# FFN-down of a gated spectral mixer: which chunks of the FFN rows lie in the large tile, and at which byte the tiles begin

## The chip, the cores and the metric

The kernel runs on one core of one Trainium2 chip. The metric is device time in microseconds (us), the median over several executions. The numbers below come from those executions and from one execution that the hardware profiler took.

## The reference

A spectral mixer `a` and a gated FFN `b` work on the same input `x` (2 batches, 4096 tokens, 640 features, float32), and a sigmoid gate per token mixes them.

```python
g = sigmoid((x * gate_w).sum(-1, keepdims=True))
a = irfft2(mlp(rfft2(x)))                               # 4 blocks of 160 features, soft threshold
b = (gelu(x @ w_gate) * (x @ w_up)) @ w_down            # 640 -> 1728 -> 640
return g * a + (1 - g) * b
```

The change lies in the last product of `b`, the FFN-down: for 8192 tokens, 1728 FFN rows are contracted to 640 features.

## The kernel before, in words

All products run on TensorE in a split form: a float32 operand is written as a high part (a copy by ScalarE, `high`, L285) and a rest (a subtraction on VectorE, `low`, L288), and a product is three matmuls: high x high, rest x high, high x rest. `split` does one of each. A matmul has a stationary operand, which is loaded into the array ahead of it, and a moving operand, which streams through. Matmuls that add into one PSUM bank follow one another; `run` (L473) issues those of the FFN and `mms`/`mm3` (L304) most others.

The program has four stretches: (1) FFN-up with gate (`quad`, 256 columns a matmul; between quads stand the steps of the first transform, `a_step`, L624); (2) the spectral MLP; (3) the inverse transforms; (4) the FFN-down with the second inverse transform (`inv2`) and the mixing. The order of the instructions is written out by hand: lists of hooks say between which matmul groups a load, a split or a sum is issued, and each engine works through its own in that order.

*FFN rows.* The 1728 rows are 14 chunks of 128, the last half filled (its other half is zero). `h_store` writes each chunk of the hidden values to a DRAM tensor `hD` with 14 columns of 128 for each token group, `h_load` reads them back in the FFN-down.

*The FFN-down* (`down`) uses a Strassen-like form with seven block products: chunk `j` is paired with `j + 6` for j below 6, and chunk 12 with 13. A unit `i` (32 of them) is two groups of 128 tokens. Each of its blocks, in the order a11, s2, s3, s1, a12, a22, s4, contracts seven chunks, j = 0 to 6, against weights of the forms b11, t2, t3, t1, b21, t4, b22. A chunk takes three matmuls of 320 columns (two for the half-filled j = 6 in a12, a22, s4, called `HALF`), so that a unit has 144.

The stationary operands are the tiles `ho`, which `h_op` makes two blocks ahead: five chunks in one `big` tile, two chunks in two `still` tiles. The five are chunks 0 to 4 (6 to 10), the two are 5 and 12 (11 and 13); the blocks take them in this order. The moving operands are the weights `wx`; `wd_load` brings them in pieces of four, three or two parts into `big`, `mid` and `small` tiles, where they stay.

*Pools.* For each partition, `small` has 17 tiles of up to 640 floats, `big` 17 of 1344, `still` 12 of 256, `mid` 13 of 1024, `tiny` 10. A `big` tile of `ho` uses 1280 of its 1344 floats and a `mid` tile of `wx` 960 of 1024, so that these may begin at an offset; `off` counts floats of 4 bytes. `small` and `still` are used in full by `wx` and `ho`. `off` is 15 for `wx` in `big`, 31 for `wx` and for the operands of `inv2` in `mid`, and 0 for `ho`. The seven weight sets take 14 of the 17 `big` tiles.

*First transform.* `f1_load` brings its tables into `big` tiles at offset 0. In `a_step` they are the stationary operand and `xs`, in a `small` tile, the moving one, 320 columns.

Of the kernel before, what the change touches and what calls it, by code (L numbers as in the profile page):

```python
# [11 lines left out]
F32R = mybir.dt.float32r  # L12
# [3 lines left out]
P = 128  # L16
# [198 lines left out]
def spectral_mix_kernel(ctx: ExitStack, tc: tile.TileContext, a):  # L215
# [3 lines left out]
    def dr(t, off, ap):  # L219
        return bass.AP(tensor=t.tensor, offset=t.offset + off, ap=ap)  # L220
# [11 lines left out]
    def small(shape, dt=F32, name="small"):  # L232
        return pool[0].tile(shape, dt, name=name, tag="small", bufs=17)

    def view(t, shape, off):

        n = math.prod(shape[1:])
        t = t[:, off:off + n]
        if len(shape) == 3:
            return t.rearrange("p (a b) -> p a b", a=shape[1])  # L240
        if len(shape) == 4:
            return t.rearrange("p (a b c) -> p a b c", a=shape[1], b=shape[2])
        return t

    def big(shape, dt=F32, name="big", off=0):
        return view(pool[1].tile([P, 1344], dt, name=name, tag="big", bufs=17), shape, off)

    def still(shape, dt=F32, name="still"):
        return pool[2].tile(shape, dt, name=name, tag="still", bufs=12)
# [4 lines left out]
    def tiny(shape, dt=F32, name="tiny"):  # L254
        return pool[5].tile(shape, dt, name=name, tag="tiny", bufs=10)

    ld = nc.sync.dma_start
    late = []

    def st(dst, src):  # L260
        late.append((dst, src))
# [11 lines left out]
    hD = dram.tile([64, P, 14 * P], F32, name="hD")  # L273
# [10 lines left out]
    def high(dst, src, scale=1.0):  # L284
        nc.scalar.activation(dst, src, AF.Copy, scale=scale)  # L285

    def low(dst, src, hi, eng=nc.vector):
        eng.tensor_sub(dst, src, hi.bitcast(F32))  # L288

    def split(dst_h, dst_l, src, eng=nc.vector):  # L290

        high(dst_h, src)
        low(dst_l, src, dst_h, eng)
# [177 lines left out]
    def run(dst, ops, first=True):  # L471
        for i, (l, r) in enumerate(ops):
            nc.tensor.matmul(dst, l, r, start=first and i == 0, stop=i == len(ops) - 1, skip_group_check=True)  # L473

    def h_store(tp, t, h):
        st(dr(hD, 4 * tp * P * 14 * P + t * P, [[14 * P, P], [P * 14 * P, 4], [1, P]]),
           h.rearrange("p (t n) -> p t n", t=4))

    def x_of(o, *names):
# [11 lines left out]
    def quad(key, t, hook, fresh):  # L491
# [50 lines left out]
        def half4():  # L542
            run(C, prod(w["u2"], x_of(o, "t4")), first=False)
            nc.vector.tensor_add(u2, C, u2)  # L544
            h = v["h"]
            nc.vector.tensor_mul(h[:, 256:], h[:, 256:], v["u4"])
            nc.vector.tensor_mul(h[:, :256], u2, p1)
            h_store(key[1], t, h)
# [34 lines left out]
    F1, XR, XS, GW = {}, {}, {}, []  # L583

    def f1_load(q):
        m = min(5, 17 - 5 * q)
        F1[q] = big([P, 5, 2, P], F32R, name="f1")
        for x in (slice(0, 1), slice(1, m)):
            nc.gpsimd.dma_start(F1[q][:, x], a["f1"][:, 5 * q + x.start:5 * q + x.stop])

# [426 lines left out]
    V, WM, S2, HR, HO = {}, {}, {}, {}, {}  # L1017
    HALF = ("a12", "a22", "s4", "b21", "t4", "b22")
# [67 lines left out]
    def wd_load(j, part):  # L1086
        d = WM.setdefault(j, {})
        kinds = {(5, 2): ((big, 4), (small, 2)), (6, 1): ((small, 2),) * 2, (6, 2): ((small, 2),) * 3}.get(
            (j, part), (((big, 4),) if part < 2 else ((mid, 3),) * 2))
        at_, parts = 4 * part, []  # L1090

        def go(t, k, n):
            ld(t.rearrange("p h d -> p (h d)").bitcast(F32), dr(wdf[j], 320 * k, [[14 * 320, P], [1, 320 * n]]))
        for i, (kind, n) in enumerate(kinds):
            off = {} if kind is small else {"off": 31} if kind is mid else {"off": 15}
            t = kind([P, n, 320], F32R, name="wx", **off)
            if part < 2 or i == 0:
                go(t, at_, n)
            else:
                later.append(lambda t=t, k=at_, n=n: go(t, k, n))  # L1100
            parts += [t[:, k] for k in range(n)]
            at_ += n
        for k in range(len(parts) // 2):
            d[FORMS[2 * part + k]] = parts[2 * k], parts[2 * k + 1]
# [17 lines left out]
    def h_load(i, part):  # L1122

        b, na = c_seq[i]
        d = HR.setdefault(i, {})
        for r, k in (((0, 0), (1, 0)), ((1, 1), (0, 1)))[part]:
            blk = (32 * b + toks(na)[r]) * P * 14 * P
            t, u = small([P, 5, P], name="hraw"), tiny([P, 2, P], name="hraw")
            d[f"a{r + 1}{k + 1}"] = t, u
            ld(t, dr(hD, blk + 6 * k * P, [[14 * P, P], [1, 5 * P]]))  # L1130
            ld(u, dr(hD, blk + (6 * k + 5) * P, [[14 * P, P], [(7 - 5 * k) * P, 2], [1, P]]))

    def h_s3(i, eng=nc.vector):
        d = HR[i]
# [20 lines left out]
        d["s4"] = d.pop("s2")  # L1155

    def h_op(i, name, eng=nc.vector):
        t = big([P, 5, 2, P], F32R, name="ho")
        uh, ul = (still([P, 2, P], F32R, name="ho") for k in range(2))
        src, six = HR[i].pop(name) if name in ("s1", "s3", "s4", "a22") else HR[i][name]  # L1160
        split(t[:, :, 0], t[:, :, 1], src, eng)
        if name == "a22":
            high(uh[:, 0], six[:, 0])
            high(ul[:64, 1], six[:64, 1])
            high(uh[64:, 1], six[:64, 1])
            low(ul[:, 0], six[:, 0], uh[:, 0], eng)
            low(uh[:64, 1], six[:64, 1], ul[:64, 1], eng)
        elif name in HALF:
            high(uh, six)
            low(ul[:, 0], six[:, 0], uh[:, 0], eng)  # L1170
            low(uh[64:, 1], six[:64, 1], uh[:64, 1], eng)
        else:
            high(uh, six)
            low(ul, six, uh, eng)
        HO[i, name] = [(t[:, j, 0], t[:, j, 1]) for j in range(5)] + [(uh[:, j], ul[:, j]) for j in range(2)]

    def inv2(i):

# [156 lines left out]
    for k, (b, n2) in enumerate(a_seq):  # L1335
        i, j = steps_a[k]
        sp = A_POINTS[keys[i][0]][j]
        if k == 0:
            back(i, sp[0] - 12, lambda: f1_load(0))
        back(i, sp[0] - 9, lambda b=b, n2=n2: a_load(b, n2))  # L1340
        for s, f in zip(sp, (lambda b=b, n2=n2: a_split(b, n2, 0), lambda b=b, n2=n2: a_split(b, n2, 1),
                             lambda b=b, n2=n2: a_gate(b, n2), lambda b=b, n2=n2: a_step(b, n2, 0),
                             lambda b=b, n2=n2: a_step(b, n2, 1))):
            back(i, s, f)
        if k in (17, 37, 57):
            back(i, sp[4], lambda q=(k + 3) // 20: f1_load(q))
# [24 lines left out]
    for i, key in enumerate(keys):  # L1371
        gr, tp = key
# [3 lines left out]
        if nxt:  # L1376
# [3 lines left out]
            for k, s in enumerate((5, 8, 11, 14, 16, 18, z + 1, z + 4, z + 6) if gr < 2 else  # L1380
                                  (6, 9, 13, 17, 21, z + 1, z + 2, z + 3, z + 3, z + 5)):
                if k < 9 or nxt[0] == 2:
                    f0, f1, f2_ = x_prep(nxt, k)
# [62 lines left out]
    def events(i, j):  # L1446
        for f, *args in todo.get((i, j), []):
            f(*args)
    wl = lambda part, *js: [(wd_load, j, part) for j in js]
    fin = {S - 14: wl(0, 0),  # L1450
           S - 13: wl(0, 1),
# [6 lines left out]
           S - 4: [(c_load, 0), *wl(1, 0, 1)],  # L1458
           S - 3: [(v_load, 1), *wl(2, 2)],
           S - 2: [(h_load, 0, 0), *wl(1, 2), (h_load, 0, 1), (wd_later,)],  # L1460
           S - 1: [(c_split, 0), (h_op, 0, "a11"), *wl(1, 3, 4, 5), *wl(0, 6), (h_s3, 0, nc.gpsimd), (h_s2, 0, nc.gpsimd), (c_load, 1)],
           S: [(h_op, 0, "s2"), (c_split, 1), (h_s1, 0, nc.gpsimd)],
           S + 1: [*wl(2, 3), (flush,), *wl(2, 4), (wd_later,)]}
# [30 lines left out]
    for i in range(len(c_seq)):  # L1494
# [4 lines left out]
        def step(k):  # L1499
            def f():  # L1500
                if (i, k) == (0, 0):
                    wd_load(5, 2)
                    wd_later()
                if (i, k) == (0, 2):
                    ahead.update(inv2(1))
                if k in (0, 5):
                    flush()
                if k < 5:
                    if k == 0:
                        h_s4(i)  # L1510
                    h_op(i, ("s3", "s1", "a12", "a22", "s4")[k])
                if n is not None:
                    if k in (1, 2):
                        h_load(n, k - 1)
                    if k == 2 and n > 1:
                        c_load(n)
                        v_load(n)
                    if k == 4:
                        h_s3(n, nc.gpsimd)
                        h_s2(n, nc.gpsimd)  # L1520
                    if k == 5:
                        h_op(n, "a11")
                        if n > 1:
                            c_split(n)
                    if k == 6:
                        h_op(n, "s2")
                        h_s1(n, nc.gpsimd)
            return f
# [23 lines left out]
```

## Time and profile before

| What | us |
|---|---|
| median of 3 runs (2538.0 to 2538.25) | 2538.02 |
| the profiled execution: its own time | 2536.59 |
| the profiled execution: span from first to last instruction | 2534.8 |
| TensorE busy within the span | 2526.3 |
| VectorE busy | 1992.5 |
| ScalarE busy | 1500.8 |
| GpSimd busy | 365.1 |

The span is shorter than the execution's time by what lies around the first and the last instruction. The page of the profile gives busy time of each engine, the span in 40 slices with the granted TensorE clock (PEclk), the DMA queues, the chain of work that ended last (followed back from the last instruction to what released each step), the costliest groups of instructions by line, and the DMA issues. PE is TensorE's matmuls, PEld its weight loads, DVE is VectorE, ACT ScalarE, POOL GpSimd, SP SyncE, which issues most DMAs. Since matmuls are pipelined, the duration of one (about 300 ns) is longer than the distance between two starts; the distance is read from the chain, as a piece's time divided by its count.

### The profile page before, as it was taken

The page shows a single profiled execution, that of the slowest core. Times are in us where ns is not written, and L with a number is a line of the kernel's source. Part 1 is how long each engine was busy: PE and PEld are TensorE (multiplying, and loading weights), DVE is VectorE, ACT ScalarE, POOL GpSimd, SP SyncE. Part 2 cuts the span into 40 slices and gives each one's busy share as a digit, 9 for nine tenths or more (in the row PEclk, how much of TensorE's full clock was granted, in tenths as well). Part 3 has the DMA queues.
Part 4 walks back from the last instruction along what each step waited for, and adds up shares of the span by engine and source line. Part 5 has one row for each costly group of instructions (what it writes and reads, how often), then busy time and mean ns, then how long its engine had stood idle before and what let it go on. Part 6 is the DMA issues. An engine that isn't in the chain of part 4 may idle for free.

```text
span 2534.8 us, 54450 instructions
## 1 busy us (share of the span) xinstructions
PE 2526.3 (100%) x20351; PEld 2523.1 (100%) x20351; DVE 1992.5 (79%) x4194; ACT 1500.8 (59%) x3552; POOL 365.1 (14%) x378
## 2 busy tenths in 40 slices
PE   9999999999999999999999999999999999999999
PEld 9999999999999999999999999999999999999999
DVE  7666677777778777787547887888898988889987
ACT  6555555666656566666546877787644445444553
POOL 0000000000000000000001111111233333333332
PEclk9999999999999999999999999999999999999999
DMA  6555556676667677777667554548744444444442
GB/s 233 184 199 191 184 203 214 213 235 209 223 206 261 190 237 246 244 233 225 214 199 219 156 154 137 158 144 272 274 149 151 157 156 132 140 151 156 152 133 101
DMA packets 338427, 483.82 MB, mean 191 GB/s; under 512 B 25772, under 2 KB 209196, under 8 KB 338164
## 3 DMA queue, kind: packets, MB, share of 16 engines
q1 hardware_dynamic: 321172, 437.16, 53.4%
q0 software_dynamic: 16128, 41.56, 4.8%
q8 instruction: 160, 2.62, 0.4%
q10 hardware_dynamic: 864, 1.64, 0.2%
q14 instruction: 103, 0.84, 0.1%
HBM read 300.62 MB, written 179.64 MB: 189 GB/s over the span
## 4 chain that ended last, share of the span: by engine, by line
PE 99%; DVE 1%; issue 0%; DMA 0%; ACT 0%; POOL 0%; SPq 0%; DVEq 0%; ACTq 0%
PE bank L473 79%; PE bank L304 14%; PE bank L766 3%; PE bank L624 1%; PE bank L823 1%; PE bank L822 1%; PE bank L825 0%; DMA xraw<-in_xT_dram 0%; PE bank L921 0%; PE bank L974 0%; DVE s2s L288 0%; DVE ys L288 0%; POOL hs L1143 0%; PE bank L895 0%; DVE ho L288 0%
## 5 line engine op out<-in xcount | busy, mean ns | idle before, releaser
L473 PE MATMUL bank<-xo,w 128*128 128x256 f32 x11749 | 1358.0, 276 | 0.4 <-DVE xo L288 0.3
L473 PEld LDWEIGHTS bank<-xo,w 128*128 128x128 f32 x11749 | 1349.8, 188 | 0.9 <-DVE xo L288 0.8
L473 PE MATMUL bank<-wx,ho 128*128 128x320 f32 x4608 | 672.0, 306 | 0.2 <-DVE ho L288 0.2
L473 PEld LDWEIGHTS bank<-wx,ho 128*128 128x128 f32 x4608 | 667.8, 188 | 0.5 <-DVE ho L288 0.5
L496 ACT ACTIVATE u<-bank 128x256 f32<-128x256 f32 x408 | 156.4, 383 | 301.3 <-PE bank L473 245.3
L285 ACT ACTIVATE ho<-hraw 128x640 fp32r<-128x640 f32 (+3 forms) x384 | 179.3, 517 | 148.1 <-PE bank L473 144.2
L288 DVE TENSOR_TENSOR ho<-hraw,ho 128x640 fp32r<-128x640 f32 (+3 forms) x384 | 225.8, 635 | 3.0 <-ACT ho L285 2.0
L544 DVE TENSOR_TENSOR u<-bank,u 128x256 f32<-128x256 f32 x204 | 86.3, 423 | 163.6 <-PE bank L473 162.1
L288 DVE TENSOR_TENSOR xo<-xraw,xo 128x512 fp32r<-128x512 f32 x209 | 143.0, 684 | 15.8 <-ACT xo L285 14.4
L288 DVE TENSOR_TENSOR xs<-xr,xs 64x640 fp32r<-64x640 f32 x128 | 105.0, 820 | 63.4 <-ACT xs L285 58.2
L626 DVE TENSOR_TENSOR as<-bank,as 64x320 f32<-64x320 f32 x256 | 113.8, 483 | 28.0 <-ACT as L625 26.2
L304 PE MATMUL bank<-wm,h 128*128 128x320 f32 x768 | 132.5, 307 | 0.0
L285 ACT ACTIVATE xo<-xraw 128x512 fp32r<-128x512 f32 x209 | 129.3, 627 | 1.5 <-DVE w L288 0.3
L497 ACT ACTIVATE h<-bank 128x256 f32<-128x256 f32 x204 | 77.2, 378 | 73.9 <-PE bank L473 66.0
L496 ACT ACTIVATE p<-bank 128x256 f32<-128x256 f32 x204 | 78.1, 383 | 68.7 <-PE bank L473 63.9
L304 PEld LDWEIGHTS bank<-wm,h 128*128 128x128 f32 x768 | 114.8, 188 | 0.2 <-DVE h L801 0.2
L288 DVE TENSOR_TENSOR s2s<-s,s2s 128x320 fp32r<-128x320 f32 x128 | 113.8, 946 | 0.4 <-ACT s2s L285 0.4
L625 ACT ACTIVATE as<-bank 64x320 f32<-64x320 f32 x256 | 96.7, 427 | 29.4 <-PE bank L624 27.3
L1136 POOL TENSOR_TENSOR hraw<-hraw 128x640 f32<-128x640 f32 x64 | 78.7, 1246 | 241.9 <-DMA hraw<-hD 116.5
L576 POOL MEMSET h<- 64x512 f32 x16 | 8.4, 522 | 712.3 <-DVE xo L288 338.5
L1199 ACT ACTIVATE uu<-bank,gs 128x320 f32<-128x320 f32 x120 | 54.2, 524 | 87.9 <-PE bank L304 85.6
L285 ACT ACTIVATE ho<-hs 128x640 fp32r<-128x640 f32 (+1 forms) x128 | 67.0, 571 | 66.1 <-PE bank L473 61.4
(167 smaller groups left out, 3491.1 us busy)
## 6 DMA issues: line engine op xcount, KB each, us to landing
xo<-xD SPq DMA_DIRECT2D x124, 512.0 KB
xraw<-in_xT_dram SPq DMA_DIRECT2D x225, 256.0 KB
hD<-h SPq DMA_DIRECT2D x224, 256.0 KB
hraw<-hD SPq DMA_DIRECT2D x128, 320.0 KB
xD<-xo POOLq DMA_DIRECT2D x64, 512.0 KB, 3.9
xr<-in_x_dram SPq DMA_DIRECT2D x64, 320.0 KB
scr<-as SPq DMA_DIRECT2D x64, 320.0 KB
sc<-scr SPq DMA_DIRECT2D x64, 320.0 KB
```

Source lines behind the costliest of these rows:

```text
L285: nc.scalar.activation(dst, src, AF.Copy, scale=scale)
L288: eng.tensor_sub(dst, src, hi.bitcast(F32))
L304: nc.tensor.matmul(dst, l, r, start=i == 0, stop=i == len(ops) - 1)
L473: nc.tensor.matmul(dst, l, r, start=first and i == 0, stop=i == len(ops) - 1, skip_group_check=True)
L496: copy = lambda d, s_: nc.scalar.activation(d, s_, AF.Copy)
L497: gelu = lambda d, s_: nc.scalar.activation(d, s_, AF.Gelu_apprx_tanh)
L544: nc.vector.tensor_add(u2, C, u2)
L625: nc.scalar.activation(stg[hi, cs], pa[lo, :320], AF.Copy)
L626: nc.vector.tensor_add(stg[hi, cs], pa[hi, :320], stg[hi, cs])
L766: nc.tensor.matmul(pz[:, kp * P:(kp + 1) * P], SC[b, c, kp][:, o:o + P], ft, start=True, stop=True)
L1136: eng.tensor_sub(d["a21"][k], d["a11"][k], d["a21"][k])
L1199: nc.scalar.activation(uu[n2][:, cs], pe[:, :320], AF.Copy, scale=gs[:, b, 0, n2:n2 + 1])
```

## The change

- `H_ORDER` gives the columns of `hD` another order: 0, 1, 2, 5, 12, 3, 4, then 6, 7, 8, 11, 13, 9, 10. `h_store` writes to it. `h_load` reads five columns and then the next two, in one run each; before, the two lay apart and were two runs.
- `h_op` puts chunks 0, 1, 2, 5 and 12 (6, 7, 8, 11 and 13) into the `big` tile and chunks 3 and 4 (9 and 10) into the `still` tiles. The blocks still take the chunks in the order of before. The half-filled chunk is now the fifth of the large tile, and the special treatment of the half moves there.
- The `big` tile of `ho` begins at offset 49 (196 bytes).
- The weights in `big` and `mid` tiles begin at offset 0 and 16 (0 and 64 bytes), and stay at 15 and 31 for j = 3 and 4.
- The tables of the first transform begin at offset 49 too.

```diff
+    H_ORDER = [0, 1, 2, 5, 12, 3, 4, 6, 7, 8, 11, 13, 9, 10]
+
     def h_store(tp, t, h):
-        st(dr(hD, 4 * tp * P * 14 * P + t * P, [[14 * P, P], [P * 14 * P, 4], [1, P]]),
+        st(dr(hD, 4 * tp * P * 14 * P + H_ORDER.index(t) * P, [[14 * P, P], [P * 14 * P, 4], [1, P]]),
            h.rearrange("p (t n) -> p t n", t=4))
...
     def f1_load(q):
         m = min(5, 17 - 5 * q)
-        F1[q] = big([P, 5, 2, P], F32R, name="f1")
+        F1[q] = big([P, 5, 2, P], F32R, name="f1", off=49)
...
-            off = {} if kind is small else {"off": 31} if kind is mid else {"off": 15}
+            off = {} if kind is small else {"off": (31 if j in (3, 4) else 16) if kind is mid else 15 if j in (3, 4) else 0}
...
-            ld(t, dr(hD, blk + 6 * k * P, [[14 * P, P], [1, 5 * P]]))
-            ld(u, dr(hD, blk + (6 * k + 5) * P, [[14 * P, P], [(7 - 5 * k) * P, 2], [1, P]]))
+            ld(t, dr(hD, blk + 7 * k * P, [[14 * P, P], [1, 5 * P]]))
+            ld(u, dr(hD, blk + (7 * k + 5) * P, [[14 * P, P], [1, 2 * P]]))
...
     def h_op(i, name, eng=nc.vector):
-        t = big([P, 5, 2, P], F32R, name="ho")
+        t = big([P, 5, 2, P], F32R, name="ho", off=49)
         uh, ul = (still([P, 2, P], F32R, name="ho") for k in range(2))
-        src, six = HR[i].pop(name) if name in ("s1", "s3", "s4", "a22") else HR[i][name]
-        split(t[:, :, 0], t[:, :, 1], src, eng)
-        if name == "a22":
-            high(uh[:, 0], six[:, 0])
-            high(ul[:64, 1], six[:64, 1])
-            high(uh[64:, 1], six[:64, 1])
-            low(ul[:, 0], six[:, 0], uh[:, 0], eng)
-            low(uh[:64, 1], six[:64, 1], ul[:64, 1], eng)
-        elif name in HALF:
-            high(uh, six)
-            low(ul[:, 0], six[:, 0], uh[:, 0], eng)
-            low(uh[64:, 1], six[:64, 1], uh[:64, 1], eng)
-        else:
-            high(uh, six)
-            low(ul, six, uh, eng)
-        HO[i, name] = [(t[:, j, 0], t[:, j, 1]) for j in range(5)] + [(uh[:, j], ul[:, j]) for j in range(2)]
+        five, two = HR[i].pop(name) if name in ("s1", "s3", "s4", "a22") else HR[i][name]
+        high(t[:, :, 0], five)
+        if name in HALF:
+            low(t[:, :4, 1], five[:, :4], t[:, :4, 0], eng)
+            if name == "a22":
+                high(t[:64, 4, 1], five[:64, 4])
+                high(t[64:, 4, 0], five[:64, 4])
+                low(t[:64, 4, 0], five[:64, 4], t[:64, 4, 1], eng)
+            else:
+                low(t[64:, 4, 0], five[:64, 4], t[:64, 4, 0], eng)
+        else:
+            low(t[:, :, 1], five, t[:, :, 0], eng)
+        split(uh, ul, two, eng)
+        a_, b_ = [(t[:, k, 0], t[:, k, 1]) for k in range(5)], [(uh[:, k], ul[:, k]) for k in range(2)]
+        HO[i, name] = a_[:3] + b_ + a_[3:]
```

## The prediction

> **What bounds the kernel now.** I read the page first: busy times, then the chain that ended last.
>
> ```profile
> span 2534.8 us, 54450 instructions
> PE 2526.3 (100%) x20351; PEld 2523.1 (100%) x20351; DVE 1992.5 (79%) x4194; ACT 1500.8 (59%) x3552; POOL 365.1 (14%) x378
> PEclk9999999999999999999999999999999999999999
> DMA packets 338427, 483.82 MB, mean 191 GB/s; under 512 B 25772, under 2 KB 209196, under 8 KB 338164
> PE 99%; DVE 1%; issue 0%; DMA 0%; ACT 0%; POOL 0%; SPq 0%; DVEq 0%; ACTq 0%
> ```
>
> TensorE is busy all the time at full granted clock and is 99% of the chain. Nothing off TensorE can pay; a change pays only if a matmul starts sooner after the one before it, or if TensorE waits less. All waits of TensorE are in the view of waits, cut to it:
>
> ```profile
> PE bank L1299 <- DVE zero L1297: 1.2, 1, 1.2
> ...
> PE bank L473 <- DVE xo L288: 0.3, 1, 0.3
> PE bank L473 <- DVE ho L288: 0.2, 1, 0.2
> ```
>
> In the FFN-down (32 units of 144 matmuls) it waits 0.2 us once, for an operand that VectorE finishes late. What is left is the distance from one matmul's start to the next. The chain by time shows it, first over whole units, then cut to pieces of the unit that starts at 2442.61 us:
>
> ```profile
> 2420.21 20.83 PE bank L473 x144
> 2441.04 1.73 PE bank L304 x12
> 2442.77 20.83 PE bank L473 x144
> ```
> ```profile
> 2442.77 6.07 PE bank L473 x42
> ```
> ```profile
> 2448.84 14.76 PE bank L473 x102
> ```
>
> A unit's FFN-down takes 20.83 us, 144.65 ns a matmul; the 12 matmuls of `inv2` between units, also 320 columns wide, 1.73/12 = 144.2 ns. The blocks a11 and s2 (42 matmuls) take 144.5 ns each; the other 102, 144.7 ns.
>
> The code says what differs. Every tile size in these pools is a multiple of 64 bytes, so I count places in bytes past a multiple of 64. All stationary operands (`ho`) lie at 0. Moving operands (`wx`) in `big` and `mid` tiles lie at 60 (`off` 15 and 31), those in `small` tiles at 0. The small ones hold b22 of chunk pair 5 and t3, t1, b21, t4, b22 of pair 6: 3+3+3+2+2+2 = 15 matmuls a unit, all among the 102. The inverse transform (L304) has its moving operand at 60 throughout. The one other line with 320 columns and its moving operand at 0 is the first transform, L624:
>
> ```profile
> L624 PE MATMUL bank<-xs,f x256: 306/308/360, 66.3 to 1227.3; 128*128 128x320 f32 x128
> ```
> ```profile
> L473 PE MATMUL bank<-wx,ho x2540: 302/305/312, 2099.7 to 2499.9; 128*128 128x320 f32 x196
> ```
>
> (min/median/max ns of one, the second cut to 2100 to 2500 us.) A moving operand at 0 costs 308 - 305 = 3 ns by these rows; by the pieces above, (14.76 - 102 x 0.1445)/15 = 1.4 ns, though the rounding of the pieces to 10 ns makes that 0 to 3. I take 2.2 ns, half way, and keep 0 and 3. So far the trace cannot say whether it is the moving operand's own place that counts, or its distance from the stationary operand that is being loaded for the next matmul at the same time: all of those are at 0 before.
>
> **The change part by part.**
>
> *Places in the large tile.* `ho` moves to 196 bytes, that is 4 past a multiple of 64; its weights (chunks j = 0, 1, 2, 5, 6) move from 60 to 0, so the distance of +4 stays. The j = 3, 4 chunks sit in `still` tiles at 0 and keep weights at 60. The 15 small-tile matmuls, whose stationary was in `still`, now have it in the large tile, so their distance goes from 0 to +4. If distance counts, 15 meetings at distance 0 go. But a matmul runs beside the load for the next one, so new meetings come: the last product of j = 2 (weights at 0) beside the load of j = 3 (at 0), in each of 7 blocks, and the end of s4 beside the first load of `inv2`: 8 at distance 0. And 8 at a distance of +8: j = 4 beside the load of j = 5, and `inv2`'s last beside a11's first. No row shows +8; bounds 0 and 3 ns by the rows above (a gain isn't excluded, but nothing in these rows is near one), I take 1 because +4 costs nothing over its own mean. Sum: (15 - 8) x 2.2 - 8 x 1 = 7 ns a unit, x32 = 0.2 us gained. Ends: a gain of at most 144 x (144.65 - 144.2) x 32 = 2.1 us, if every matmul ran like those of `inv2`; a loss of 8 x 3 x 32 = 0.8 us, if small tiles cost nothing and the new meetings cost 3.
>
> *First transform's tables* at 196 bytes: each of 128 steps has two matmuls; the first runs beside a load of the same table (now at distance 4), the second beside a quad's weight at 0, as before. 128 x 2.2 = 0.3 us gained (0 to 0.4).
>
> *Operand making.* For a12, a22, s4, VectorE's 640-element subtraction becomes 512, a 128-element one becomes 256, the half-height one stays; ScalarE has one 128-element copy of a22 grow to 256. Steady rows:
>
> ```profile
> L288 DVE TENSOR_TENSOR ho<-hraw,ho 128x640 fp32r<-128x640 f32 x89 | 78.0, 876 | 2.0 <-ACT ho L285 2.0
> L285 ACT ACTIVATE ho<-hraw 128x640 fp32r<-128x640 f32 x89 | 65.5, 736 | 84.2 <-PE bank L473 84.2
> L285 ACT ACTIVATE ho<-hraw 128x256 fp32r<-128x256 f32 x71 | 28.8, 406 | 0.8 <-DVE ho L288 0.8
> L288 DVE TENSOR_TENSOR ho<-hraw,ho 128x256 fp32r<-128x256 f32 x53 | 22.1, 417 | 0.0
> L288 DVE TENSOR_TENSOR ho<-hraw,ho 128x128 fp32r<-128x128 f32 x36 | 15.1, 420 | 0.0
> L285 ACT ACTIVATE ho<-hraw 64x128 fp32r<-64x128 f32 x36 | 10.8, 301 | 0.4
> ```
>
> The 512-element one lies between 417 and 876 ns; the pair costs VectorE 0.46 us less to equal per block. ScalarE gains 406 - 301 = 0.1 us a unit. Both lie beside TensorE. The count of instructions stays.
>
> *Release of the large tile.* ScalarE's 84 us of idle ahead of these copies is a wait for TensorE to let go of a large tile: 14 of 17 hold weights, three rotate. Until now TensorE leaves the tile at j = 4, six matmuls (0.87 us) before the block's end (five in a half-height block); now at the end, and the `still` tiles sooner. So the makers start up to 0.87 us later, while VectorE's last part (the `still` pair) is wanted at j = 3 instead of j = 5. The tightest block is s3. VectorE in its unit:
>
> ```profile
> 2445.40 1.15 DVE L1154 TENSOR_TENSOR hs<-hraw,hs 128x640 f32<-128x640 f32 x2
> 2446.47 2.23 DVE L288 TENSOR_TENSOR ho<-hraw,ho 128x640 fp32r<-128x640 f32 x4
> 2448.87 0.49 DVE L1230 TENSOR_TENSOR e<-bank,e 128x320 f32<-128x320 f32 x1 [0.18 <-PE bank L473]
> ```
>
> Four operations in 2.23 us, two of them s3's (half, 1.1 us, to about 2447.6); TensorE starts s3 at 2448.7 (the piece of 102, whose time is 0.16 later than the matmul's start). That is 1.1 us of margin for the `still` pair and more for the large tile, so a delay of 0.87 us stays covered in the steady units. In the first two units VectorE is behind (the wait of 0.2 us above). There the delay can come out: 0 to 0.9 us once; below nothing too, to -0.2, as `still` tiles come free earlier. I take 0.2, what it costs now again.
>
> *DMAs.* The 128 loads of the two-chunk part read 1 KB runs instead of two of 512 bytes:
>
> ```profile
> hraw<-hD SPq DMA_DIRECT2D x128, 128.0 KB
> ```
>
> 128 x 128 = 16384 packets fewer of 338427. The stores of `h` write other columns with the same run length, and the weight loads the same bytes at another start. Nothing is added to SP's or POOL's queue, none is moved past another. DMA is 0% of the chain; priced at 0.
>
> *Sum:* -0.2 - 0.3 + 0.2 = -0.3 us. The profiled execution took 2536.59 us (span 2534.8); the runs' median is 2538.02, 1.4 us above. So 2536.3 beside the former, **2537.7** beside the latter. Own range -2.1 - 0.4 - 0.2 to +0.8 + 0.9: 2535.3 to 2539.7.
>
> **The rivals.**
>
> *A: the moving operand's own place decides (slower).* Then 102 matmuls a unit read at 0 instead of 15: 87 x 2.2 x 32 = 6.1 us, 2544.1; with 1.4 to 3 ns, 2541.9 to 2546.4. It passes 0.2% (5.1 us) at 1.8 ns. For it: in this trace only the moving place ever varies. Against: a start that is off by 4 bytes has no plain reason to be quicker by itself, a clash with the load beside it has. [...]
>
> *B: the new pairing is quicker than the old (faster).* Quads, 256 columns, run at
>
> ```profile
> 604.16 8.52 PE bank L473 x75
> ```
> ```profile
> L473 PE MATMUL bank<-xo,w 128*128 128x256 f32 x11749 | 1358.0, 276 | 0.4 <-DVE xo L288 0.3
> ```
>
> 113.6 ns; by width, 142.0 for 320. If the 102 went there, (144.5 - 142.0) x 102 x 32 = 8.2 us, 2529.8. Against: quads have distance 0, and 320 columns there are no better (308 above). [...]
>
> *C: the later release becomes a wait (slower).* Decides once the makers' delay eats more than s3's 1.1 us; every 0.2 us beyond comes 32 times, 6.4 us, 2544.4. Against: 0.87 us, and less work on VectorE.
>
> *D: places don't matter at all,* the difference of 3 ns being the neighbours' doing: 2538.0.
>
> **How the numbers follow.** Forecast 0.51, D 0.20, A 0.16, B 0.08, C 0.05. Faster or slower by over 0.2% (5.1 us, about what a measurement of this kernel can tell from no change): B gives 0.08 faster; C and three quarters of A 0.17 slower; the rest 0.75 same. The forecast and D hold 0.71 in 2535.3 to 2539.7; the range takes in the lower two thirds of A and ends at 2545.0 above, and at 2534.8 below.
>
> **What would show it.** The unit's piece in the chain: 20.82 us if right, 21.02 for A, 20.57 for B, 20.83 for D; for C, a wait of L473 for `ho` in every unit. L624's median falls from 308 towards 306 if distance counts, stays for A and D. Packets fall to 322043. The prediction is wrong if the x144 piece moves by more than 0.05 us.

## The result, and the profile after

The changed kernel is slower: 2557.62 us, median of 6 runs (2555.47 to 2560.63), beside 2538.17 (2538.0 to 2539.3) for the kernel before in the same comparison; ratio 1.0075, 95% interval 1.0065 to 1.0086. Forecast were 2537.7 us and, with three chances in four, no change. The profiled execution took 2555.47 us. From the page of its profile (span, busy times, granted clock, DMA packets, and the groups of L473):

```profile
span 2553.3 us, 54441 instructions
PE 2544.7 (100%) x20351; PEld 2541.1 (100%) x20351; DVE 2021.0 (79%) x4194; ACT 1507.8 (59%) x3552; POOL 373.6 (15%) x378
PEclk9999999999999999999999999999999999999999
DMA packets 322043, 483.82 MB, mean 189 GB/s; under 512 B 25772, under 2 KB 192812, under 8 KB 321780
L473 PE MATMUL bank<-xo,w 128*128 128x256 f32 x11749 | 1370.5, 278 | 0.5 <-DVE u L536 0.3
L473 PE MATMUL bank<-wx,ho 128*128 128x320 f32 x4608 | 677.6, 308 | 0.5 <-DVE ho L288 0.5
```

The same number of matmuls, at the same granted clock, keeps TensorE busy 18.4 us longer (2544.7 against 2526.3), and the span is 18.5 us longer. So hardly anything was lost to waiting; the matmuls follow each other at larger distances. The larger part is in the FFN-up, which the change touches through the tables of the first transform and through the columns that `h_store` writes: its matmuls (`xo,w`) went from 1358.0 to 1370.5 us. The FFN-down's (`wx,ho`) went from 672.0 to 677.6, by this row of the groups before:

```profile
L473 PE MATMUL bank<-wx,ho 128*128 128x320 f32 x4608 | 672.0, 306 | 0.2 <-DVE ho L288 0.2
```

In the FFN-down TensorE waits once, as before (view of waits, after):

```profile
PE bank L473 <- DVE ho L288: 0.5, 1, 0.5
```

Where the FFN-up lost it is seen in the chain of work in order of time (start, length in us, line, count of matmuls). L624 is a step of the first transform, between quads of L473. First before, from 66.50 us on, and the piece behind the last step:

```profile
66.50 0.29 PE bank L624 x2
66.80 3.55 PE bank L473 x31
70.34 0.29 PE bank L624 x2
70.64 70.06 PE bank L473 x618
140.70 0.29 PE bank L624 x2
...
293.09 139.21 PE bank L473 x1228
...
1227.64 17.36 PE bank L473 x153
```

Then after, where the step's line is L626:

```profile
66.82 0.29 PE bank L626 x2
67.12 3.63 PE bank L473 x31
70.75 0.29 PE bank L626 x2
71.04 72.79 PE bank L473 x618
143.84 0.29 PE bank L626 x2
144.13 3.56 PE bank L473 x31
147.69 0.29 PE bank L626 x2
147.98 72.79 PE bank L473 x618
...
224.80 71.10 PE bank L473 x619
...
300.02 139.22 PE bank L473 x1228
...
1240.15 4.90 PE bank L473 x43
```

The steps themselves take what they took (0.29 us). But the 618 quad matmuls that follow the step at 70.75 us take 72.79 us instead of 70.06: 117.8 ns each instead of 113.4, all the way to the next step, 73 us later. Nothing that these 618 read or load has moved. After the step at 143.84 us the stretch is quick again, after the next one slow. So the stream of quads has two lasting cadences with the same operands. Before, all 128 steps leave it quick (113.3 to 113.4 ns a quad, by the starts). After, each step turns it from one cadence into the other, so that slow and quick pieces take turns to the end of the stretch:

```profile
439.53 2.83 PE bank L473 x24
442.37 0.30 PE bank L626 x2
442.66 11.38 PE bank L473 x100
454.04 0.29 PE bank L626 x2
454.33 2.13 PE bank L473 x18
```

These three pieces took 2.74, 11.37 and 2.06 us before. One more thing sets the cadence: where two matmuls of 128 columns stand among the quads, the stream is quick behind them. After the change there are 11 such pairs behind the first step, two of which meet it slow. One of the two is in the x619 piece, after its 206th matmul; by the starts the piece runs at 117.8 ns ahead of the pair and at 113.4 behind. The x618 pieces have none.

The two x618 pieces, 2.73 us each, and the x619 one with 0.91 make 6.4 us of the 6.9 by which the x1228 piece starts later (300.02 against 293.09); that piece runs at the old 113.4 ns. Further on the short pieces (24, 18 and 39 matmuls) run at some 118 ns, and behind the last step the kernel is 12.5 us late (1240.15 against 1227.64).

In the FFN-down the chain shows units of

```profile
2392.23 20.99 PE bank L473 x144
2413.23 1.73 PE bank L304 x12
2414.96 21.00 PE bank L473 x144
```

20.83 before: 0.167 us more (worked out from the starts of the matmuls, mean of 27 units: 20.995 and 20.828), in 32 units 5.3 us. The 12 matmuls of `inv2` stayed at 1.73. Together 12.5 + 5.3 = 17.8 of the span's 18.5 us.

### The profile page after: what moved, and what is told of

It is laid out like the page before. It is cut to its first block, busy times and chain, and to the rows that moved or that the text cites. A ratio compares the mean times of both kernels' runs of the same rounds, so it can differ in the third digit from the quotient of the medians.

```text
span 2553.3 us, 54441 instructions
## 1 busy us (share of the span) xinstructions
PE 2544.7 (100%) x20351; PEld 2541.1 (100%) x20351; DVE 2021.0 (79%) x4194; ACT 1507.8 (59%) x3552; POOL 373.6 (15%) x378
## 2 busy tenths in 40 slices
DMA packets 322043, 483.82 MB, mean 189 GB/s; under 512 B 25772, under 2 KB 192812, under 8 KB 321780
## 4 chain that ended last, share of the span: by engine, by line
PE 97%; DMA 1%; DVE 1%; ACT 1%; issue 0%; SPq 0%; POOL 0%; ACTq 0%; DVEq 0%; POOLq 0%
PE bank L473 77%; PE bank L304 13%; PE bank L768 3%; PE bank L626 1%; PE bank L825 1%; PE bank L824 1%; DMA rl<-in_w1l_dram 0%; DMA scr<-is 0%; DMA s<-scr 0%; DMA hraw<-hD 0%; PE bank L827 0%; DMA xraw<-in_xT_dram 0%; PE bank L923 0%; DVE ho L288 0%; PE bank L976 0%
## 5 line engine op out<-in xcount | busy, mean ns | idle before, releaser
L473 PE MATMUL bank<-xo,w 128*128 128x256 f32 x11749 | 1370.5, 278 | 0.5 <-DVE u L536 0.3
L473 PEld LDWEIGHTS bank<-xo,w 128*128 128x128 f32 x11749 | 1361.6, 188 | 1.3 <-DVE xo L288 0.6
L473 PE MATMUL bank<-wx,ho 128*128 128x320 f32 x4608 | 677.6, 308 | 0.5 <-DVE ho L288 0.5
L473 PEld LDWEIGHTS bank<-wx,ho 128*128 128x128 f32 x4608 | 673.2, 188 | 1.0 <-DVE ho L288 1.0
L285 ACT ACTIVATE ho<-hraw 128x640 fp32r<-128x640 f32 (+2 forms) x384 | 187.2, 532 | 171.8 <-PE bank L473 168.0
L288 DVE TENSOR_TENSOR ho<-hraw,ho 128x256 fp32r<-128x256 f32 (+3 forms) x384 | 239.7, 665 | 18.0 <-ACT ho L285 15.5
L460 POOL DMA_DIRECT2D xD<-xo x64 | 34.2, 535 | 481.6 <-DVE xo L288 472.6
L288 DVE TENSOR_TENSOR ho<-hs,ho 128x256 fp32r<-128x256 f32 (+3 forms) x160 | 99.1, 636 | 5.4 <-ACT ho L285 3.4
```

The lines of the kernel that those rows point to most:

```text
L460: nc.gpsimd.dma_start(xD[key[1]][:, kept], XM.pop((key, name)).rearrange("p h n -> p (h n)").bitcast(F32))
```

## The experiments

Places are given here in bytes modulo 128, moving operand first, stationary second: FFN-down before (60, 0), after (0, 68) for the five chunks in the large tile and (60, 0) for the two in `still`; quads (64, 0). Letters in the quoted expectations are names of theories, set out there. Each time stands beside the median of the kernel before in the same comparison; intervals are of the ratio, 95%. Distances inside a block are worked out from the starts of successive matmuls, averaged over units.

**Which part costs what.** The theories: the tables upset the neighbouring quads and the places in the FFN-down cost the rest; rivals, the new order of the chunks with its later release, or the moving operand's own place.

*Tables back to 0, the rest changed.*

```diff
-        F1[q] = big([P, 5, 2, P], F32R, name="f1", off=49)
+        F1[q] = big([P, 5, 2, P], F32R, name="f1")
```

> The changed kernel with the first transform's tables back at offset 0; the FFN-down as changed. Theory P (a stationary load whose place is 4 bytes off turns TensorE's stream from one lasting cadence to another, so that the 256-column matmuls behind each step of the first transform run at 118 instead of 113 ns): the 12.5 us that the FFN-up's matmuls gained in busy time go, the FFN-down's units stay at 20.99 us, about 2538.2 + 32 x 0.165 = 2543.5 us. Rival Q (the FFN-up is slower for another reason, its stores to other columns of hD or the state of the chip): 2555 or more, FFN-up matmuls still in the slow cadence.

2545.15 us beside 2539.32, ratio 1.0022 (1.0013 to 1.0032). Its chain:

```profile
72.73 70.06 PE bank L473 x618
...
2383.46 21.00 PE bank L473 x144
```

The quads are quick again, the units stay at 21.00.

*The reverse: only the tables at 196 bytes, in the kernel before.*

> The kernel before with nothing changed but the tables of the first transform at 196 bytes. Theory P: 2538.2 + 13 = 2551 us, with stretches of 118 ns behind every other step; FFN-down units 20.83 us. Rival Q: 2538 us. The recorded forecast for this part: 2537.9 us.

2552.6 us, ratio 1.0051 (1.0034 to 1.0068), 13.3 us more:

```profile
67.34 3.63 PE bank L473 x31
70.98 0.29 PE bank L624 x2
71.27 72.79 PE bank L473 x618
...
2391.47 20.83 PE bank L473 x144
```

The slow cadence comes with the tables alone, and the units stay at 20.83. The two parts add up: 13.3 + 5.8 = 19.1 us against 19.5 for the whole change.

*The new order of chunks alone, all offsets as before.*

```diff
-            off = {} if kind is small else {"off": (31 if j in (3, 4) else 16) if kind is mid else 15 if j in (3, 4) else 0}
+            off = {} if kind is small else {"off": 31} if kind is mid else {"off": 15}
-        t = big([P, 5, 2, P], F32R, name="ho", off=49)
+        t = big([P, 5, 2, P], F32R, name="ho")
```

(and the tables at 0)

> The changed order of the chunks (hD columns, operand making, two-chunk part at j = 3 and 4) with all places as before: tables and ho at 0, weights at 15 and 31. Theory P and the theory that only places cost: FFN-down units 20.83 us within 0.02, whole 2538.2 us within 1. Rival R (the later release of the large tile or the new operand making costs): units longer, or waits of TensorE for ho, up to 2543.5 us.

2539.81 us, 1.0003 (0.9994 to 1.0012), and the unit:

```profile
2380.07 20.83 PE bank L473 x144
```

The order, the making of the operands, the later release and the packets cost nothing that can be measured. The profiled execution (2542.13 us) shows by its starts that a slow cadence can come without the tables: at the step at 923 us three successive starts are 182 and 222 ns apart (113 and 148 at other steps), and the 666 quad matmuls from there to the next pair of 128 columns run at 117.8 ns, 13 further steps between them. So with the tables at 0 a step keeps the cadence that it finds, slow or quick; with the tables at 196 bytes it turns it.

*Tables at 0, and all weights at 0 or 64 bytes* (`{"off": 16} if kind is mid else {"off": 0}`).

> Changed kernel with tables back at 0 and the weights of j = 3 and 4 at 0 and 64 bytes too, so that no weight lies at 60: j = 0, 1, 2, 5, 6 at distance +4, j = 3, 4 at distance 0. Theory T (the loss comes from the change of place in the middle of a block, after which j = 5 and 6 run at about 147 instead of 145 ns): j = 5 and 6 fall to 145 ns as j = 0 to 2, j = 3 and 4 rise to about 146.7; unit about 20.93 to 20.97 us, 2541 to 2543 us. Theory A (own place of the moving operand): no matmul is left at 60, all 144 at 145.5 to 147, unit 21.0 to 21.1 us, 2544 to 2547 us.

2546.68 us, 1.0028 (1.0018 to 1.0039):

```profile
2384.26 21.06 PE bank L473 x144
```

This is the unit that theory A named, not T's 20.93 to 20.97: j = 5 still runs at 147.8 ns. (A is decided below, by moving `ho` alone.) The pairing (0, 0) of j = 3 and 4 runs at some 146.7 ns, and the slow matmuls behind each change from `still` to the large tile remain.

**Is it the 4 bytes past a multiple of 64, or the place?** Before with the tables at 192 (`off=48`) and at 200 bytes (`off=50`):

> The kernel before with the tables at 192 bytes, a multiple of 64. Theory P (the 4 bytes past a multiple of 64 flip the cadence): no slow stretch, FFN-up matmuls 113.3 ns between steps, 2538 us. Rival (any move of the tables, the later end of the tile or its load does it): slow stretches as in the run with the tables alone, 2551 us.

> The kernel before with the tables at 200 bytes, 8 past a multiple of 64. If the flip comes from a start at an odd 4-byte word: 2538 us, no slow stretch. If from any start that is no multiple of 16 or 64 bytes: slow stretches, about 2551 us.

2551.27 us, 1.0044 (1.0024 to 1.0063), and 2552.04, 1.0049 (1.0029 to 1.0069); both show the slow x618 pieces, first at 192, then at 200 bytes:

```profile
71.36 72.79 PE bank L473 x618
```
```profile
71.80 72.79 PE bank L473 x618
```

So the odd 4 bytes are not the cause. In both, as with the tables alone at 196, each step turns the cadence but one, at 932 to 933 us, at which two starts are 175 to 299 ns apart. With the tables at 256 (`off=64`) and 128 bytes (`off=32`):

> The kernel before with the tables at 256 bytes. The tables at 192, 196 and 200 bytes all flipped the cadence, so the 4 bytes were not the cause. Theory M (what flips it is a stationary operand at another place within 256 bytes than the stationary operands around it, all of which lie at multiples of 256 here): no flip, FFN-up matmuls at 113.3 ns between steps, about 2538 to 2539 us. Rival N (the later place in the tile or its later end, whatever the remainder): flips, about 2551 us.

> The kernel before with the tables at 128 bytes. If places count within 256 bytes: flips, 2551 us. If within 128 bytes: none, 2538 to 2539 us. Rival N: flips.

2539.53, 0.9999 (0.9987 to 1.001), and 2538.39, 0.9994 (0.9983 to 1.0005), beside 2538.95. At 128 bytes:

```profile
67.53 3.55 PE bank L473 x31
71.08 0.29 PE bank L624 x2
71.37 70.06 PE bank L473 x618
```

Of the places tried for the steps' stationary operand, 192, 196 and 200 bytes upset this stream (72.79 us for 618 matmuls), 0, 128 and 256 do not (70.06): modulo 128 that is 64, 68 and 72 against 0.

**Does the moving operand's own place decide in the FFN-down (rival A)?** New order, tables at 0, weights at 60 as before, only `ho` at 196; the same with `ho` at 32 bytes (`off=8`); and the kernel before with the weights at 28 bytes (`off` 7 and 23):

> Changed order of the chunks, ho at 196 bytes, all weights left at 15 and 31 (60 past a multiple of 64), tables at 0: the moving operand's place is that of before, the stationary one's distance is +8 in the large tile. Theory A (own place of the moving operand decides): 144.4 ns as before, unit 20.83 us, 2538 us. Theory S (the stationary operand's odd word costs whatever the moving one's place): 145 ns or more in j = 0, 1, 2, 5, 6, unit 20.9 us or more, 2540.5 us or more. Theory D (distance +4 against other distances decides): unlike both, most likely slower than the changed kernel's 20.99 us.

> Changed order of the chunks, ho at 32 bytes, weights at 15 and 31 as before, tables at 0: all stationary starts even 8-byte words, the small-tile weights at 0 meet stationary operands at 32. Theory A: 146.7 ns stay for the small tiles, unit 20.83 us. Theory D (equal places meet, any distance helps): small tiles fall to 144.4, unit 20.78 us, 1.6 us less in all. Theory S: no loss in j = 0, 1, 2, since 32 bytes is no odd word.

> The kernel before with the FFN-down's weights in big and mid tiles at 28 and 92 bytes instead of 60 and 124, everything else as before; all stationary operands at 0. Theory D64 (the distance within 64 bytes counts, and only +4 is known to be good): another cadence than 144.4, between 143.3 and 146.7, unit 20.7 to 21.1 us. Theory A (any moving place off the multiple of 64 is good): 144.4 and 20.83 us as before. The open question is whether 60 is special.

2545.77 us beside 2539.44 (1.0024, 1.0012 to 1.0035), 2542.4 (1.0011, 1.0000 to 1.0022) and 2541.9 beside 2538.95 (1.0016, 1.0005 to 1.0027). The units, one row of each kernel's chain, in this order:

```profile
2383.17 21.03 PE bank L473 x144
```
```profile
2404.31 20.91 PE bank L473 x144
```
```profile
2401.95 20.96 PE bank L473 x144
```

In the first no moving operand has moved from its place of before, and the unit is as slow as after the change: at (60, 68) the matmuls run at 146.7 ns. So A is out: the moving operand's own place does not decide alone. The second, 20.91, fits none of its three theories. In the third only the moving operands moved, and that costs too: either place, moved alone, changes how a matmul runs (146.7 and 145.4 ns, for 144.4).

**Do the changes between the tiles cost?** After, with tables at 0, blocks s2, s1 and a22 take chunks 3 and 4 first and the others take them last, so that four changes from `still` to the large tile are left of eight:

```diff
-            for j, (hh, hl) in enumerate(h):
+            for j in ((0, 1, 2, 5, 6, 3, 4), (3, 4, 0, 1, 2, 5, 6))[a_ in ("s2", "s1", "a22")]:
+                hh, hl = h[j]
```

> The changed kernel with tables back at 0, and the blocks taking their chunks in turn as large tile then still tiles and still tiles then large tile, so that the way from a still tile (at 0) to a large tile (at 196) is gone about half as often. Theory M/T (the loss in j = 5 and 6 is what a change of the stationary operand's place leaves behind): the slow matmuls (147 ns and over) appear only after the remaining changes, unit 20.91 to 20.94 instead of 20.99 us. Theory S (the chunks 5 and 6 are slow by their own places): unit stays at 20.99 us.

2543.6 us beside 2538.95, 1.0011 (1.0 to 1.0023). Unit:

```profile
2382.07 20.95 PE bank L473 x144
```

20.948 against 20.995, that is 12 ns for each change taken away (a little less than theory M/T's 20.91 to 20.94 asks for, but not S's 20.99). In the kernel after, the six distances behind a change are 144, 149, 149, 144, 151 and 145 ns in most blocks; with half of the changes such slow matmuls stand behind the remaining ones only. The 167 ns that a unit lost are then, by the starts: eight changes, some 95 ns; the large tile's 102 matmuls at 145.4 ns instead of 144.4, some 100; less some 30 that a unit of before took over 144.4 ns a matmul, its small tiles' slow meetings above all.

**Distance within 128 or 64 bytes?** Five kernels, each beside 2539.3. In the kernel before, the filler in the pool is 64 floats instead of 48, which moves every `mid` and `tiny` tile by 64 bytes, so that the quads' moving operand lies at 0:

```diff
-    pool[3].tile([P, 48], F32, name="gap", tag="gap", bufs=1)
+    pool[3].tile([P, 64], F32, name="gap", tag="gap", bufs=1)
```

> The kernel before with the gap ahead of the mid and tiny tiles widened from 192 to 256 bytes, so that mid tiles begin at a multiple of 128 instead of 64 past one: every stationary operand of the program then lies at a multiple of 128 (before, h of the spectral MLP lay at 64). Moving operands in mid tiles shift by 64 too. Theory M (a change of the stationary operand's place within 128 bytes leaves a slow stretch): the stretches of 118 ns in the spectral MLP's 256-column matmuls (13200 on in order) go, L304's z and h groups lose some 3 to 4 us in all, 2535 us, unless the quads' moving operands at 0 instead of 64 cost something, which no run shows. Rival (the MLP's slow stretches come from its float32 matmuls of the second transform or its waits): nothing changes there, 2538.5 us.

2618.05 us, 1.0308 (1.0292 to 1.0323):

```profile
L473 PE MATMUL bank<-xo,w 128*128 128x256 f32 x11749 | 1431.8, 283 | 0.3 <-DVE xo L288 0.3
74.28 74.16 PE bank L473 x618
```

(its groups and its chain) 120.0 ns a quad matmul at (0, 0) against 113.4 at (64, 0), everywhere; TensorE's busy time in the quads grew by 73.8 of the 78.8 us. The expectation, 2535 us, was far off, and this is the largest effect of all: the quads had stood in a good place. The weights of the FFN-down in `mid` tiles moved too, to (124, 0): a22 and s4 run at 146.7 ns there, and the unit takes 20.92 us.

In the kernel before, the spectral MLP's first stationary weights at 64 bytes (`off=16`):

> The kernel before with the first MLP layer's stationary weights at 64 bytes, the place of h within 128 bytes, so that fewer changes of place stand between the two layers; their moving operands then have distance 0 within 128 instead of 64. Theory M: fewer slow stretches, 0 to 3 us less, 2535.5 to 2538.5 us. Rival (distance within 128 of moving and stationary counts more): longer, up to 2545 us.

2540.91 us, 1.0007 (0.9997 to 1.0016), within the noise as a time; but the matmuls in question went from 115.4 to 117.8 ns (`z,wm`) and from 115.1 to 120.3 (`zl,wl`): before, the two operands lay 64 bytes apart, (64, 0), now they lie at the same place, (64, 64), and the sign is that of the quads.

After, with tables and `ho` at 128 bytes (`off=32`) and at 256 (`ho` alone, `off=64`), weights at 60:

> The change with its large tiles (ho and tables) at 128 instead of 196 bytes and all weights at 15 and 31 as before: chunks and operand making as changed, the stationary operands at a place that equals 0 within 128 bytes. Theory M: no slow stretch anywhere, units 20.83 us, 2538.5 us. Rival (a large tile that does not begin at its start costs): units above 20.9 us, 2541 us or more.

> The changed order of the chunks with ho at 256 bytes, tables at 0, weights at 15 and 31. With ho at 128 bytes the unit took 20.89 us instead of 20.83. If places within 256 bytes count in the FFN-down: 20.83 us at 256. If any large tile that does not begin at its start costs: 20.86 us or more.

2540.36 us (1.0004, 0.9994 to 1.0015) and 2539.05 (1.0002, 0.9992 to 1.0013). Units:

```profile
2402.78 20.89 PE bank L473 x144
```
```profile
2421.84 20.83 PE bank L473 x144
```

256 bytes change nothing, the matmuls' distances being those of before one by one; 128 bytes cost 0.06 us a unit, where theory M named none. In the FFN-down, then, 128 and 256 bytes are not the same place (20.89 us a unit against 20.83), which the tables had not shown.

In the kernel before, weights at 64 bytes (`off` 16 and 32), the distance that is best for the quads:

> The kernel before with the FFN-down's weights in big and mid tiles at 64 within 128 bytes instead of 60, the stationary operands at 0. The 256-column matmuls ran at 113.3 ns with 64 bytes between the two operands' places and at 120 ns with 0 (gap at 256). Theory D128 (the distance within 128 bytes counts, half of it is best): 143.3 to 144.4 ns, unit 20.65 to 20.83 us, 2533 to 2538.5 us. Rival (60 bytes, the odd word, is what made 320 columns quicker than a multiple of 64): 146.7 ns as in the small tiles, unit 21.1 us, 2547 us.

2547.9 us, 1.0034 (1.002 to 1.0047); units of

```profile
2384.63 21.13 PE bank L473 x144
```

146.7 ns a matmul, the slowest unit of all, as the rival to D128 had it. What is quickest of the places tried at 256 columns is not so at 320.

What was measured of a steady matmul, by places and width (means of the distances between starts):

| Columns | Places (moving, stationary) and ns |
|---|---|
| 256 | (64, 0) 113.4, or 117.8 once upset; (0, 0) 120.0; (64, 64) 117.8 and 120.3 |
| 320 | (60, 0) 144.4, in a22 of the kernel before 143.3; (60, 32) 145.2; (28, 0) 145.4; (0, 68) 145.4; (60, 68), (0, 0), (64, 0) and (124, 0) 146.7 |

## Why the prediction was wrong

*What bounds the kernel.* Right: the loss is all in the distance from one matmul's start to the next, on TensorE, at full granted clock.

*The tables: the step that failed most.* Priced at a gain of 0.3 us, as 128 matmuls of their own by 2.2 ns, with the sentence that the second of a step "runs beside a load ... at 0, as before". Measured alone: a loss of 13.3 us, none of it in those 256 matmuls (0.29 us a step as before; their median went from 308 to 309 ns, not towards 306).

```profile
L626 PE MATMUL bank<-xs,f x256: 307/309/313, 66.7 to 1239.8; 128*128 128x320 f32 x128
```

The neighbours were priced at nothing because their own operands stay. What lies there is a stream of 11749 matmuls with two lasting cadences, 113.4 and 117.8 ns, and with the tables at 196 bytes each step turns it from one into the other. The forecast had no term and no rival for that, so no end of its range reached it.

*Places in the large tile: mis-sized and with the wrong sign.* Forecast 0.2 us gained, at most 0.8 lost; measured 5.3 lost (5.8 by the kernel with the tables back). Two premises failed. First, the price of a new meeting: 1 to 2.2 ns at one matmul, where a change between tiles costs 12 ns spread over the next six. Second, that a distance of +4 past a multiple of 64 "stays" when both places move: (0, 68) runs at 145.4 ns, (60, 0) at 144.4. The prediction had counted places modulo 64, which nothing in the trace supported, since counted so every stationary operand stood at 0; modulo 64 hid that the two operands were 60 bytes apart modulo 128 and which of the two lay where. The small tiles' slow meetings did go, as forecast, and are a small part. The sign of being wrong that the prediction named came: the x144 piece moved by 0.17 us, not by less than 0.05.

*Operand making, release, packets:* right. The order alone gives 2539.81 beside 2539.32; the one wait for `ho` went from 0.2 to 0.5 us, 0.3 more where 0.2 more was forecast; packets fell to 322043, the number forecast.

*The rivals.* A named 21.02 us for the unit, and 20.99 to 21.00 came, but for another reason: with the moving operands where they were, the unit is 21.03. C did not come: one wait of 0.5 us. B's quicker pairing did not come; what was held against it, that the quads have distance 0, is so modulo 64 only: modulo 128 they stand at (64, 0). D fell by the first comparison. That the load's place may count, which the prediction held against A, no row of before could show, as all loads lay at 0 modulo 64; it was the author's assumption. The runs bear it out as far as the place goes: with the moving operands in their places of before, moving the stationary operand alone took the matmuls of the large tile from 144.4 to 146.7 ns. By what way it slows them, no run tells. Nor was a moving operand at a multiple of 64 bytes quicker: at (64, 0) the matmuls ran at 146.7 ns, against 144.4 at (60, 0).

*What stays open.* The runs show what a step does to the quads' cadence, turn it with the tables at 64, 68 or 72 bytes and keep it with them at 0, but not why there are two cadences, nor why this place turns them. For 320 columns there is no one rule: (0, 68) and (60, 0) have the same distance modulo 128 and differ by 1 ns; (60, 0) itself runs at 144.4 ns, but at 143.3 in a22 of the kernel before; and 128 bytes, which the quads do not notice, cost 0.06 us a unit. What makes a place count there, no run tells.

## What to carry to other kernels

When the chain is 99% TensorE, take the time between starts in each stretch and write beside it where both operands begin, modulo 256 bytes and not 64: here `ho` at 128 bytes gave units of 20.89 us, and of 20.83 at 0 and 256. Moving either operand is a change to matmuls whose other operand stays: `ho` alone at 196 bytes took them from 144.4 to 146.7 ns, the weights alone at 28 bytes to 145.4. Change places one operand at a time and read the neighbours' pieces too, above all the long streams that follow: a table used for 0.29 us at a time cost 13 us in matmuls that were not edited. A price for a place should be carried over to no other width or pair: (64, 0) gave 113.4 ns, the quickest of the places tried at 256 columns, and 146.7, among the slowest, at 320.

## What the runs showed of the hardware that was not expected

- A stream of 256-column matmuls with operands in unchanged places runs steadily at either 113.4 or 117.8 ns, and stays there for hundreds of matmuls. Two other matmuls between them turn it from one into the other when their stationary operand lies at 64, 68 or 72 bytes modulo 128, and keep it when that lies at 0; a pair of 128-column matmuls left it quick (113.4 ns behind it, 117.8 ahead). With the tables at 0, the slow cadence came too, for 666 matmuls, at one step whose starts were 182 and 222 ns apart.
- The places of the operands alone are worth 3% of this kernel: 64 bytes on the `mid` and `tiny` tiles, 120.0 against 113.4 ns a quad matmul, 2618 against 2539 us.
- At 320 columns the steady matmuls ran at 143.3 to 146.7 ns, with 64 bytes between the operands at the slow end (146.7), where at 256 columns that is the quick one (113.4 ns, against 120.0 with 0).
- At 320 columns a change of the stationary operand's place from 0 to 68 within a stream slowed the matmuls behind it, by 12 ns in all (units of 20.995 and, with four changes fewer, 20.948 us).
